# Planning a fused attention and mixture-of-experts kernel with a shared port as a lock and a margin for inputs, another seed, and softmax sums by a reduction

## The chip, the cores and the metric

One Trainium2 chip; the kernel runs on one of its cores. The metric is device time in microseconds (us) of one execution. The engines are named as in the profile: PE is TensorE, PEld its weight loads, DVE is VectorE, ACT is ScalarE, POOL is GpSimd, SP is SyncE (it issues most of the DMAs).

## What is computed

Windowed attention over 4 batches, 8 heads, 576 positions, 64 wide; its output is the input of a mixture of 8 experts (top one per token), and that of a dense block.

```python
scores = scale * np.matmul(q, k.transpose(0, 1, 3, 2))
mask = (rel >= 0) & (rel < 64)                   # rel = query position - key position
attn = exp(scores - max) / (sum(exp(scores - max)) + 1e-09)
x = (attn @ v) as 2304 rows of 512
logits = x @ w_gate + modality_bias[modality_id]
e = argmax(logits); gate_w = softmax(logits)[e]
y = gate_w * (relu(x @ w1[e]) @ w2[e])           # 8 experts, 512 -> 1024 -> 512
h = y @ w_in; out = (h - tanh(h)) @ w_out        # 512 -> 2048 -> 512
```

## The kernel before

The program has two halves. The first, `front`, does attention, routing and the experts, and it is written out in an order that a planner finds when the program is built. The second, `second`, runs the dense block over 6 chunks of 384 tokens and 16 slices each in an order fixed by hand (L1772 for `x @ w_in`, L1820 for the product with `w_out`).

The planner is the class `Flow`. Each piece of work is a Python generator that yields `Op`s: an engine (or a choice of engines) with a duration in us, the tokens it waits for, the buffers it takes. `pick` looks at every waiting `Op`, takes the engine on which something can start first, and on that engine the `Op` with the smallest priority number among those that can start within 0.05 us of the first. Priorities of 0 to 30 get a small pseudo-random addition from `nudge`, which depends on `SEED`. The generator then emits its instructions, so an engine's program order is the order in which the planner picked. On the chip every engine works through its own list in that order and waits for semaphores; the planner's own durations play no further part.

What the planner orders, with the lines that matter here:

- 16 pairs of heads (4 a batch) and 4 tails (the last 64 rows of all heads of a batch). Of a pair, PE transposes k and q (L596, L604), adds the mask and the scores (L694, L707), transposes the probabilities (L732) and multiplies with v (L746). DVE or ACT copy what PE left in PSUM (L615, L623, L380 and L382, two halves of one helper).
- The softmax, `t_soft`: DVE takes the row maximum (L774), ACT the exponentials with their sums (L777), DVE adds 1e-9 to the sums (L780) and takes reciprocals (L781), and GpSimd, or DVE, multiplies (L783). It runs 36 times.
- The routing, `route`, once a batch, when all heads of the batch are done: PE forms the logits (L885, then L902, with `lt` their transpose); DVE adds the bias and finds the one-hot `oh` of the expert in seven short instructions (L906, L907, L908, L919, L920, L921, L922); PE ranks the tokens (L926, L927, where L927 waits for `oh`); DVE and GpSimd build a table (L941 to L992).
- The experts, in five units of up to 504 tokens: unit 0 is early and needs only the first batch's table, unit 1 the third's, units 2 to 4 that of all. A unit is 96 matmuls of the first layer (L1365) and 96 of the second (L1385). `t_wsplit` cuts the weights in two parts, `wh` (L380 or L382) and `wl` (L1340), `t_hid` gives the hidden rows `hh` (L1396) and `hl` (L1399). They have the largest priority numbers, so they fill in where attention leaves an engine free.
- `t_conv` turns the dense block's weights from float64 words into float32 (L1455 to L1482), from about 150 us on.

Of the kernel before, what the change touches and what calls it, by code (L numbers as in the profile page):

```python
# [56 lines left out]
SPACE = 2.0  # L57
NUDGE, SEED = 1.0, 179
CONV0 = 14
# [85 lines left out]
class Op:  # L145
    def __init__(self, eng, deps=(), rings=(), bank=None, prio=None, wire=0.0, lag=1.6, nb=1, bias=None):
        self.eng = eng if isinstance(eng, dict) else {eng[0]: eng[1]} if eng else {}
        self.deps, self.rings, self.bank, self.prio, self.wire = deps, rings, bank, prio, wire
        self.lag, self.nb, self.bias = lag, nb, bias

# [5 lines left out]
class Flow:  # L156

    LAG = dict(PE=0.3, DVE=0.17, ACT=0.2, POOL=0.15, SP=0.0)
    BIAS = dict(DVE=0.2)
    LOOK = 0.05  # L160

    def __init__(self):
        self.free = dict(PE=5.8, DVE=5.0, ACT=5.0, POOL=8.0, SP=1.6)
        self.wire, self.th, self.n, self.floor = 0.0, [], 0, 0.0
        self.bank = [Tok(0.0) for _ in range(8)]

# [32 lines left out]
    def nudge(self, n):  # L199
        x = (n + 1) * (2 * SEED + 1) * 2654435761 % 2**32  # L200
        return NUDGE * ((x ^ x >> 15) * 2246822519 % 2**32 >> 8) / 2**24

    def pick(self):
        best = {}
        for th in self.th:
            op = th[3]
            t = self.ready(op)
            if t is None:
                continue
            t = max(t, th[4])  # L210
            if not op.eng:
                return None, t, th
            bias = op.bias or self.BIAS
            e = min(op.eng, key=lambda e: max(self.free[e], t) + op.eng[e] + (len(op.eng) > 1) * bias.get(e, 0.0))
            best.setdefault(e, []).append((max(self.free[e], t), th))
        assert best, "nothing can go on"
        e = min(best, key=lambda e: min(s for s, _ in best[e]))
        lo = min(s for s, _ in best[e]) + self.LOOK
# [4 lines left out]
        s, th = min((x for x in best[e] if x[0] <= lo), key=lambda x: prio(x[1]))  # L223
        return e, s, th

    def run(self):
        while self.th:
            e, s, th = self.pick()
            op, r = th[3], Done()
            r.e, r.s, r.rel = e, s, [g.take() for g in op.rings]  # L230
            r.t = s
            if e:
                end = s + op.eng[e]
                self.free[e] = end
                r.t = end + self.LAG[e]
                if op.wire:
                    self.wire = max(self.wire, end) + op.wire
                    r.t = self.wire + op.lag
                elif e == "POOL" and op.lag > 2:
                    r.t = end + op.lag  # L240
            else:
                th[4] = s
            if op.bank is not None:
                free = sorted((b for b in op.bank if self.bank[b].t is not None), key=lambda b: self.bank[b].t)
                r.bs = free[: op.nb]
                r.bts = [Tok() for _ in r.bs]
                r.bt = r.bts[0]
                for b, t in zip(r.bs, r.bts):
                    self.bank[b] = t
            r.tok = Tok(r.t)  # L250
            self.step(th, r)


class Kernel:
# [132 lines left out]
    def front(self):  # L387
# [93 lines left out]
    def t_load(self):  # L481
# [19 lines left out]
        def v(pi):  # L501
            b, hp = divmod(pi, 4)
            h0 = 2 * hp
            r = yield Op(("SP", 1.3), rings=[R["va"]], prio=1.25 * pi + 0.3, wire=W256)
            va = at.tile([128, 4, 2, 64], F32, name="va", bufs=NVA)
            for h in range(2):
                nc.sync.dma_start(va[:, :, h, :], ap["v"][b, h0 + h, 0:512, :].rearrange("(c p) d -> p c d", p=128))
            vb = at.tile([128, 3, 2, 64], F32, name="vb", bufs=NVA)
            self.raw["v", pi] = va, vb, r.rel[0]
            self.tk("va", pi).t = r.t  # L510
            here = Tok(r.t + 1.0)
            r = yield Op(("POOL", 0.53), [here], prio=1.25 * pi - 0.5)
            nc.gpsimd.tensor_copy(vb[0:64], va[0:64, 1:4])
            t, e, d = (r.t, "DVE", 0.35) if self.behind(r) else (r.t, "POOL", 0.53)
            r = yield Op((e, d), [here], prio=-30 if e == "POOL" else 1.25 * pi - 0.5)
            self.eng(r).tensor_copy(vb[64:128], va[64:128, 0:3])
            self.tk("vb", pi).t = max(t, r.t)
# [250 lines left out]
    def t_soft(self, key, ps, P, bs, tok):  # L768
        nc, at = self.nc, self.at
        r = yield Op(("DVE", 0.6), [tok])  # L770
        nm = at.tile([128, 4], F32, name="nm", bufs=8)
        sm = at.tile([128, 4], F32, name="smm", bufs=8)
# [6 lines left out]
        r = yield Op(("DVE", 0.36), [r.tok])  # L779
# [97 lines left out]
    def route(self, b):  # L877
# [25 lines left out]
        r = yield Op(("DVE", 0.65), [r.tok])  # L903
        Lg = rt.tile(sh, F32, name="Lg")
# [8 lines left out]
        te = r.tok  # L913
        r = yield Op(("DVE", 1.1))
        cand = rt.tile(sh, F32, name="cand")
# [22 lines left out]
        tp = r.tok  # L938
        r = yield Op(("DVE", 0.53), [te])
        se = rt.tile([128, n], F32, name="se")  # L940
# [3 lines left out]
        for t in range(t0, t1):  # L944
            self.flow.add(self.t_after(r.tok, self.t_xrow(t)), -6 + 0.01 * t)
        r = yield Op(("DVE", 0.35), [tp])
        ccn = rt.tile([128, E], F32, name="ccn")
# [4 lines left out]
        elif b == B - 1:  # L952
            self.flow.add(self.unit_table(r.tok), -9)
        r = yield Op(("DVE", 1.4), [tp])
        rk = cand
# [269 lines left out]
    def t_late(self):  # L1225
        we, self.es_we = self.pool("we", 1)
        for n in range(NLATE):
# [9 lines left out]
            self.nc.scalar.activation(self.wH[t], w, AF.Copy)  # L1237
            r = yield Op(dict(DVE=0.75, POOL=1.3), [r.tok], bias=dict(POOL=0.6))
            self.eng(r).tensor_tensor(lo, w, self.wH[t].bitcast(F32), op=ALU.subtract)
# [90 lines left out]
    def t_wsplit(self, i, s, w, tok, rel):  # L1330
        nc, mo, R = self.nc, self.mo, self.rings
        r = yield Op(dict(ACT=0.52, DVE=0.46), [tok], [R["wh"]])
# [108 lines left out]
    def t_conv(self, n, t):  # L1441
# [17 lines left out]
        tb = r.tok  # L1459
        yield Op(("DVE", 0.5), [ta])  # L1460
        v.tensor_scalar(x, x, bits(0x38000000), bits(0x47EFFFFF), op0=ALU.max, op1=ALU.min)
        yield Op(("DVE", 0.5))
        v.tensor_scalar(a, a, 0x07FFFFFF, 3, op0=ALU.bitwise_and, op1=ALU.logical_shift_left)
        r = yield Op(("DVE", 0.68))
        v.scalar_tensor_tensor(a, hi, -0x40000000, a, op0=ALU.bitwise_and, op1=ALU.bitwise_or)
        rr.t = max(r.t, tb.t)
        if t not in self.wH:
            r = yield Op(("POOL", 1.5), [r.tok, tb])
# [4 lines left out]
        r = yield Op(("POOL", 1.5), [r.tok, tb], [R["cw"]])  # L1473
        rw = r.rel[0]
# [502 lines left out]
```

## Time and profile before

| | |
|---|---|
| runs | 743.62, 743.67, 746.39 us; median 743.67 |
| the profiled execution | 745.83 us, span from first to last instruction 744.0 us |
| TensorE's mean granted clock | 0.992 of full speed |
| busy, share of the span | PE 97%, PEld 84%, DVE 78%, ACT 68%, POOL 43% |
| chain of work that ended last, by engine | PE 86%, DVE 7%, POOL 2%, issue 2%, ACT 1%, DMA 1% |
| HBM | 103 GB/s over the span |

The profile gives for each engine the time it was busy and, for each idle stretch, what ended it. Ends of matmuls are modelled, so PE can look busy without running at its full rate; the rate is read from how long equal pieces of work take in the chain of waits. Times in a timeline row are start and duration; what stands in brackets is how long the engine had been idle and who ended that.

### The profile page before, as it was taken

How to read it: one execution, taken by the hardware profiler on the slowest of the kernel's cores; microseconds unless marked ns; L12 is line 12 of the kernel's file. 1: busy time of each engine (PE TensorE's matmuls, PEld its weight loads, DVE VectorE, ACT ScalarE, POOL GpSimd, SP SyncE). 2: the span in 40 equal slices, each digit the busy share in tenths (PEclk: the TensorE clock that was granted, in tenths of full speed). 3: DMA queues.
4: the chain of work that ended last, by engine and by line, in shares of the span. 5: the costliest groups of instructions: out<-in, count | busy, mean ns of one | idle time of the engine just before them, and what ended most of it. 6: DMA issues, size and time to landing. Idle time of an engine off the chain costs nothing.

```text
span 744.0 us, 14477 instructions
## 1 busy us (share of the span) xinstructions
PE 723.3 (97%) x4939; PEld 627.8 (84%) x4939; DVE 581.5 (78%) x1095; ACT 507.9 (68%) x1222; POOL 322.3 (43%) x355
## 2 busy tenths in 40 slices
PE   7998999999999999999999999999999999999995
PEld 4777877788888887899998989899998989999894
DVE  6999985999999877758999996767677676767663
ACT  5887885667666555638887777667676766767672
POOL 6786673543433422214685442334244333424222
PEclk9999999999999999999999999999999999999998
DMA  8987864688786875641010110101010000001001
GB/s 187 221 199 160 201 177 121 206 246 247 225 258 212 261 244 175 187 131 30 1 43 1 43 33 11 39 7 41 1 44 22 21 15 30 23 0 43 1 0 47
DMA packets 119249, 77.30 MB, mean 104 GB/s; under 512 B 54968, under 2 KB 112332, under 8 KB 119166
## 3 DMA queue, kind: packets, MB, share of 16 engines
q1 hardware_dynamic: 114822, 66.38, 31.9%
q0 software_dynamic: 3264, 9.63, 4.1%
q8 instruction: 41, 0.67, 0.4%
q10 hardware_dynamic: 1080, 0.28, 0.2%
q14 instruction: 42, 0.34, 0.2%
HBM read 62.10 MB, written 14.16 MB: 103 GB/s over the span
## 4 chain that ended last, share of the span: by engine, by line
PE 86%; DVE 7%; POOL 2%; issue 2%; ACT 1%; DMA 1%; DVEq 0%; POOLq 0%; ACTq 0%
PE ps_g L1772 26%; PE ps_q L1820 26%; PE bank L1385 14%; PE bank L1365 12%; PE bank L746 1%; PE bank L1290 1%; DVE nm L774 1%; ACT P L777 1%; PE bank L732 1%; DMA kr<-in_k 1%; PE bank L707 1%; PE bank L857 1%; PE bank L596 1%; DVE kT L623 1%; DVE qT L615 1%
## 5 line engine op out<-in xcount | busy, mean ns | idle before, releaser
L1803 POOL TENSOR_TENSOR gl<-gv,gh 128x384 fp32r<-128x384 f32 x95 | 101.9, 1073 | 168.6 <-ACT gh L1802 166.6
L1820 PE MATMUL ps_q<-H,gl 128*128 128x512 f32 x288 | 114.0, 396 | 0.0
L1790 DVE SCALAR_TENSOR_TENSOR gv<-gu,ps_g 128x384 f32<-128x384 f32 x94 | 51.7, 550 | 79.5 <-ACT gt L1785 79.2
L1820 PE MATMUL ps_q<-H,gh 128*128 128x512 f32 x288 | 113.4, 394 | 0.0
L1802 ACT ACTIVATE gh<-gv 128x384 fp32r<-128x384 f32 x96 | 50.2, 523 | 91.0 <-issue 85.4
L1794 DVE COPY_PREDICATED gv<-gm,gt 128x384 f32<-128x384 int32 x96 | 77.2, 804 | 11.0 <-DVE gv L1793 1.4
L1793 DVE SCALAR_TENSOR_TENSOR gv<-gs,gv 128x384 f32<-128x384 f32 x96 | 68.9, 718 | 10.7 <-DVE gv L1792 0.9
L1340 DVE TENSOR_TENSOR wl<-raw,wh 128x512 fp32r<-128x512 f32 x74 | 62.3, 860 | 12.8 <-ACT wh L380 8.8
L1820 PEld LDWEIGHTS ps_q<-H,gl 128*128 128x128 f32 x288 | 54.1, 188 | 12.9 <-DVE gl L1803 0.3
L1786 ACT ACTIVATE gs<-gu,pa 128x384 f32<-128x384 f32 x96 | 59.2, 616 | 7.2 <-DVE gv L1792 7.2
L1787 ACT ACTIVATE gs<-gu,pa 128x384 f32<-128x384 f32 x96 | 59.0, 614 | 7.2 <-DVE gv L1793 7.2
L1792 DVE SCALAR_TENSOR_TENSOR gv<-gs,gv 128x384 f32<-128x384 f32 x96 | 61.9, 645 | 0.0
L1820 PEld LDWEIGHTS ps_q<-H,gh 128*128 128x128 f32 x288 | 54.1, 188 | 9.0 <-ACT gh L1802 0.2
L1789 ACT ACTIVATE gm<-gu,pth 128x384 f32<-128x384 f32 x96 | 58.4, 609 | 0.0
L1791 DVE TENSOR_TENSOR gt<-ps_g,gt 128x384 f32<-128x384 f32 x94 | 51.7, 550 | 0.0
L1784 ACT ACTIVATE gu<-ps_g 128x384 f32<-128x384 f32 x94 | 44.4, 472 | 1.6 <-PE ps_g L1772 1.6
L1785 ACT ACTIVATE gt<-ps_g 128x384 f32<-128x384 f32 x94 | 45.3, 482 | 0.0
L1396 ACT ACTIVATE hh<-bank 128x504 fp32r<-128x504 f32 (+1 forms) x40 | 22.1, 553 | 29.5 <-PE bank L1365 29.5
L380 ACT ACTIVATE ys<-bank 128x504 f32<-128x504 f32 (+1 forms) x20 | 11.1, 556 | 44.8 <-PE bank L1385 32.9
L1365 PE MATMUL bank<-xh,wh 128*128 128x504 f32 (+1 forms) x160 | 41.5, 379 | 0.0
L1365 PE MATMUL bank<-xl,wh 128*128 128x504 f32 (+1 forms) x160 | 41.4, 378 | 0.0
L380 ACT ACTIVATE wh<-raw 128x512 fp32r<-128x512 f32 x68 | 41.1, 624 | 0.0
(479 smaller groups left out, 2060.5 us busy)
## 6 DMA issues: line engine op xcount, KB each, us to landing
raw<-in_w SPq DMA_DIRECT2D x80, 256.0 KB
craw<-in_win SPq DMA_DIRECT2D x16, 512.0 KB
craw<-in_wout SPq DMA_DIRECT2D x16, 512.0 KB
va<-in_v SPq DMA_DIRECT2D x32, 128.0 KB
yd<-ys SPq DMA_DIRECT2D x16, 252.0 KB
yr<-yd SPq DMA_DIRECT2D x20, 192.0 KB
kr<-in_k SPq DMA_DIRECT2D x11, 256.0 KB
qr<-in_q SPq DMA_DIRECT2D x10, 256.0 KB
```

Of the source, the lines that this page charges most:

```text
L1340: self.eng(r).tensor_tensor(lo, w, hi.bitcast(F32), op=ALU.subtract)
L1365: nc.tensor.matmul(ps, wt[:, k, :], xt[:, k, :n], start=(k == 0 and q == 0), stop=(k == 3 and q == 2))
L1385: nc.tensor.matmul(ps, wt[:, k % 4, :], h, start=(q == 0), stop=(q == 3 * NF1 - 1))
L1772: nc.tensor.matmul(ps, w[:, c, :], x[:, c, :], start=(c == 0 and i == 0), stop=(c == 3 and i == 2))
L1786: nc.scalar.activation(s1, u, AF.Square, bias=self.pa1)
L1787: nc.scalar.activation(s2, u, AF.Square, bias=self.pa2)
L1789: nc.scalar.activation(m, u, AF.Relu, bias=self.pth)
L1792: nc.vector.scalar_tensor_tensor(v, s1, b1, v, op0=ALU.add, op1=ALU.mult)
L1793: nc.vector.scalar_tensor_tensor(v, s2, b2, v, op0=ALU.add, op1=ALU.mult)
L1794: nc.vector.copy_predicated(v, m.bitcast(I32), t)
L1803: (nc.vector if last else nc.gpsimd).tensor_tensor(gl, v, gh.bitcast(F32), op=ALU.subtract)
L1820: self.nc.tensor.matmul(self.po[t], g[:, t * 128 : t * 128 + 128], w, start=(f == 0 and i == 0), stop=(f == NF2 - 1 and i == 2),)
```

## The change

Four things are edited.

1. `SEED` is 78 instead of 179, so the pseudo-random additions to priorities differ.
2. [...] An `Op` on DVE can be marked `lock`; such an `Op` isn't started while a GpSimd `Op` runs, and a GpSimd `Op` isn't started while a marked DVE `Op` runs. With the lock, the durations that the planner assumes for many DVE steps get smaller. Routing steps, weight splits, conversions and one copy of v are marked.
3. `pick` compares an engine's candidates by the time at which they can start or, if later, by the time their inputs are there plus a margin (0.7 us on PE, 0.2 us on DVE and GpSimd). Work whose inputs have been ready for longer goes first.
4. The sums of the softmax. Eight tiles of 128x4x2 are set to 1e-9 once, at the start; ACT writes its sum into the first element of each pair, and a DVE TENSOR_REDUCE over the pair takes the place of the TENSOR_SCALAR that added 1e-9. The reciprocal stays.

```diff
-NUDGE, SEED = 1.0, 179
+NUDGE, SEED = 1.0, 78
...
+    WAIT = dict(PE=0.7, DVE=0.2, POOL=0.2)
...
+    def held(self, e, op, t):
+        o = dict(DVE="POOL", POOL="DVE").get(e)
+        if o is None or (e == "DVE" and not op.lock):
+            return t
+        a, b = self.hold[o]
+        return b if a < t + op.eng[e] and t < b else t
...
-            e = min(op.eng, key=lambda e: max(self.free[e], t) + op.eng[e] + (len(op.eng) > 1) * bias.get(e, 0.0))
-            best.setdefault(e, []).append((max(self.free[e], t), th))
+            s = {e: self.held(e, op, max(self.free[e], t)) for e in op.eng}
+            e = min(s, key=lambda e: s[e] + op.eng[e] + (len(s) > 1) * bias.get(e, 0.0))
+            best.setdefault(e, []).append((max(s[e], t + self.WAIT.get(e, 0.0)), s[e], th))
...
+                if e == "POOL" or (e == "DVE" and op.lock):
+                    self.hold[e] = s, end
...
+        self.sums, self.nsum = [at.tile([128, 4, 2], F32, name=f"sum{i}") for i in range(8)], 0
...
+        for t in self.sums:
+            nc.vector.memset(t, 1e-9)
...
-            t, e, d = (r.t, "DVE", 0.35) if self.behind(r) else (r.t, "POOL", 0.53)
-            r = yield Op((e, d), [here], prio=-30 if e == "POOL" else 1.25 * pi - 0.5)
+            t, e, d = (r.t, "DVE", 0.42) if self.behind(r) else (r.t, "POOL", 0.53)
+            r = yield Op((e, d), [here], lock=True, prio=-30 if e == "POOL" else 1.25 * pi - 0.5)
...
-            nc.scalar.activation(P[:, j, :], ps[:, j, :], AF.Exp, bias=nm[:, j : j + 1], accum_out=sm[:, j : j + 1])
+            nc.scalar.activation(P[:, j, :], ps[:, j, :], AF.Exp, bias=nm[:, j : j + 1], accum_out=sm[:, j, 0:1])
-        nc.vector.tensor_scalar(sm, sm, 1e-9, None, op0=ALU.add)
-        nc.vector.reciprocal(rc, sm)
+        nc.vector.tensor_reduce(rc, sm, op=ALU.add, axis=AX.X)
+        nc.vector.reciprocal(rc, rc)
...
-        r = yield Op(("DVE", 1.1))
+        r = yield Op(("DVE", 0.95), lock=True)
...
-        by = dict(DVE=0.8, POOL=1.2) if i < NEARLY else dict(DVE=0.8)
-        r = yield Op(by, [r.tok], [R["wl"]], bias=dict(POOL=LATE))
+        by = dict(DVE=0.62, POOL=1.2) if i < NEARLY else dict(DVE=0.62)
+        r = yield Op(by, [r.tok], [R["wl"]], bias=dict(POOL=LATE), lock=True)
```

The order of nearly every engine's instructions in the first half differs. Two places are shown. In the changed kernel line numbers are 12 to 16 higher (L906 is L922, L922 is L938, L902 is L918, L1365 is L1381).

The first is DVE in the routing of the second batch, from a copy of v to the one-hot `oh`; `nm` is a softmax maximum, `smm` a softmax sum. Before:

```order
L516 COPY vb<-va 64x384
L774 TENSOR_REDUCE nm<-bank_1536 128x4
L780 TENSOR_SCALAR smm<-smm 128x4
L781 RECIPROCAL rc<-smm 128x4
L516 COPY vb<-va 64x384
L906 TENSOR_TENSOR Lg<-bank_1613,btok 128x40
L907 TENSOR_REDUCE mx<-Lg 128x5
L908 TENSOR_TENSOR Lg<-Lg,mx 128x40
L919 TENSOR_SCALAR cand<-Lg 128x40
L920 TENSOR_TENSOR cand<-cand,iomp 128x40
L921 TENSOR_REDUCE idx<-cand 128x5
L922 TENSOR_TENSOR oh<-iom_190,idx 128x40
```

And in the changed kernel, from the third routing instruction on (a single copy of v stands directly ahead of the first, L922):

```order
L924 TENSOR_TENSOR Lg<-Lg,mx 128x40
L799 TENSOR_TENSOR P_111<-P_111,rc 128x512
L796 TENSOR_REDUCE rc<-sum_142 128x4
L797 RECIPROCAL rc<-rc 128x4
L790 TENSOR_REDUCE nm<-bank_1619 128x4
L638 COPY kT_106<-bank_1588 128x4x2x64
L394 COPY PT<-bank_1660 128x512
L935 TENSOR_SCALAR cand<-Lg 128x40
L936 TENSOR_TENSOR cand<-cand,iomp 128x40
L937 TENSOR_REDUCE idx<-cand 128x5
L938 TENSOR_TENSOR oh<-iom_206,idx 128x40
```

Six instructions of attention now stand inside the routing chain, between its third and its fourth instruction.

The second place is PE in the routing of the third batch, from the logits' transpose (`ltT`) to the ranking matmul that waits for `oh` (weights `tri`); `xh` and `xl` are rows of expert unit 0, `wh` and `wl` its weights, `P_112` probabilities. Before:

```order
L902 MATMUL bank_2144<-sel,ltT 128x8 x5
L732 MATMUL bank_2157<-idF,P_112 128x64
...
L604 MATMUL bank_2180<-idF,qr_96 128x128 x4
...
L707 MATMUL bank_2193<-kT_106,qT_105 64x128
...
L746 MATMUL bank_2230<-PT,va 64x64 x4
...
L926 MATMUL bank_2253<-cc,ones 128x40
L927 LDWEIGHTS tri
```

In the changed kernel:

```order
L918 MATMUL bank_2269<-sel,ltT 128x8 x5
L1381 MATMUL bank_2231<-xl,wh 128x504 x4
L1381 MATMUL bank_2231<-xh,wl 128x504 x2
...
L722 MATMUL bank_2305<-kT_104,qT_103 64x128
...
L761 MATMUL bank_2336<-PT,va 64x64 x4
...
L1381 MATMUL bank_2231<-xh,wl 128x504 x2
L942 MATMUL bank_2367<-cc,ones 128x40
L943 LDWEIGHTS tri
```

Eight expert matmuls now stand between the logits and the ranking; a transpose of probabilities and one of q left this place. Over the whole first half, 62 of unit 0's 96 first-layer matmuls stand ahead of the last batch's L902, against 40 before. On DVE, ahead of the last batch's routing, there are 4 more `wl` products, 2 more `hl`, 1 more cast of `wh` and 2 more copies of 128x512, and 1 copy of v and 1 row scaling fewer; of two copies the shape differs.

## Rows read from the trace of the kernel before

**Rows 1.** The page, part 1: busy time by engine.
```profile
PE 723.3 (97%) x4939; PEld 627.8 (84%) x4939; DVE 581.5 (78%) x1095; ACT 507.9 (68%) x1222; POOL 322.3 (43%) x355
```

**Rows 2.** Busy time by stage: PE, PEld, DVE, ACT, POOL, granted clock, DMA.
```profile
20.00:64.00 44.00, 41.98 (x802) 35.14 (x802) 40.56 (x113) 37.39 (x160) 33.52 (x52) 1.00 0.84 194
64.00:84.00 20.00, 18.02 (x295) 15.52 (x295) 18.50 (x50) 16.25 (x65) 14.78 (x20) 0.91 0.68 178
84.00:106.00 22.00, 20.39 (x323) 15.92 (x323) 20.14 (x57) 17.16 (x62) 13.66 (x20) 0.92 0.85 191
106.00:146.00 40.00, 38.12 (x372) 30.21 (x371) 29.20 (x84) 24.84 (x68) 20.18 (x24) 1.00 0.56 171
170.00:334.00 164.00, 164.00 (x822) 139.06 (x821) 135.59 (x218) 98.71 (x185) 51.94 (x40) 1.00 0.70 215
```

**Rows 3.** The chain that ended last, 145 to 340 us: start, duration, what.
```profile
170.14 21.97 PE bank L1365 x96
...
215.91 21.97 PE bank L1365 x96
...
333.43 6.24 PE ps_g L1772 x36
```

**Rows 4.** PE's longest waits, 6 to 146 us: total, times, longest one.
```profile
PE bank L927 <- DVE oh L922: 3.8, 3, 1.9
```

**Rows 5.** Timeline of PE at the second and third routing: start, duration, line, [idle before].
```profile
67.78 0.81 PE L902 MATMUL bank<-sel,ltT 128*128 128x8 f32 x6
...
72.73 0.18 PE L927 MATMUL bank<-oh,tri 128*128 128x40 bf16 x1 [1.91 <-DVE oh L922]
...
100.32 0.18 PE L927 MATMUL bank<-oh,tri 128*128 128x40 bf16 x1 [1.49 <-DVE oh L922]
```

**Rows 6.** Busy time and granted clock around and after these two waits.
```profile
71.00:79.00 8.00, 6.27 (x76) 5.69 (x76) 7.40 (x24) 5.68 (x14) 5.95 (x9) 0.79 0.48 134
98.00:106.00 8.00, 6.51 (x71) 4.97 (x65) 6.98 (x26) 5.90 (x18) 5.65 (x8) 0.79 0.51 135
```

**Rows 7.** Timeline of DVE at the second and third routing.
```profile
67.03 2.00 DVE L516 COPY vb<-va 64x384 f32<-64x384 f32 x1
...
72.48 0.20 DVE L922 TENSOR_TENSOR oh<-iom,idx 128x40 bf16<-128x40 f32 x1
...
98.39 0.47 DVE L919 TENSOR_SCALAR cand<-Lg 128x40 f32<-128x40 f32 x1
...
99.36 0.91 DVE L922 TENSOR_TENSOR oh<-iom,idx 128x40 bf16<-128x40 f32 x1
```

**Rows 8.** Timeline of POOL at the same two places.
```profile
67.76 1.04 POOL L783 TENSOR_TENSOR cvr<-cvr,rc 128x512 f32<-128x512 f32 x1
...
98.89 2.55 POOL L1340 TENSOR_TENSOR wl<-raw,wh 128x512 fp32r<-128x512 f32 x2
```

**Rows 9.** Timeline of DVE at the start.
```profile
6.57 0.69 DVE L623 COPY kT<-bank 128x512 f32<-128x512 f32 x1 [0.54 <-PE bank L596]
```

**Rows 10.** Groups of DVE instructions, 0 to 340 us: busy us, mean ns.
```profile
L780 DVE TENSOR_SCALAR smm<-smm 128x4 f32<-128x4 f32 x36 | 11.1, 309 | 1.5 <-ACT P L777 1.2 <-ACT cvr L777 0.3
...
L941 DVE TENSOR_REDUCE se<-ex 128x5 f32<-128x40 f32 x4 | 0.7, 175 | 0.0
```

**Rows 11.** Lines L780 and L941 each: duration in ns, least, median, most.
```profile
L780 DVE TENSOR_SCALAR smm<-smm x36: 140/170/1057, 11.2 to 116.5; 128x4 f32<-128x4 f32 x36
...
L941 DVE TENSOR_REDUCE se<-ex x4: 165/174/188, 42.9 to 129.8; 128x5 f32<-128x40 f32 x4
```

**Rows 12.** Groups of DVE instructions, 6 to 127 us.
```profile
L1340 DVE TENSOR_TENSOR wl<-raw,wh 128x512 fp32r<-128x512 f32 x5 | 3.5, 705 | 3.4 <-PE bank L1365 3.4
```

**Rows 13.** The chain that ended last, 0 to 172 us.
```profile
86.37 0.87 PE bank L707 x32
...
87.83 1.08 PE bank L746 x32
...
127.23 1.01 PE bank L902 x10
```

More of the change, by code (lines that the diff above doesn't have):

```diff
@@ L145, with __init__ @@
 class Op:
-    def __init__(self, eng, deps=(), rings=(), bank=None, prio=None, wire=0.0, lag=1.6, nb=1, bias=None):
+    def __init__(self, eng, deps=(), rings=(), bank=None, prio=None, wire=0.0, lag=1.6, nb=1, bias=None, lock=False):
         self.eng = eng if isinstance(eng, dict) else {eng[0]: eng[1]} if eng else {}
         self.deps, self.rings, self.bank, self.prio, self.wire = deps, rings, bank, prio, wire
-        self.lag, self.nb, self.bias = lag, nb, bias
+        self.lag, self.nb, self.bias, self.lock = lag, nb, bias, lock
 class Done:
@@ L164, in __init__ @@
         self.wire, self.th, self.n, self.floor = 0.0, [], 0, 0.0
+        self.hold = dict(DVE=(0.0, 0.0), POOL=(0.0, 0.0))
         self.bank = [Tok(0.0) for _ in range(8)]
@@ L213, in pick @@
             bias = op.bias or self.BIAS
-            e = min(op.eng, key=lambda e: max(self.free[e], t) + op.eng[e] + (len(op.eng) > 1) * bias.get(e, 0.0))
-            best.setdefault(e, []).append((max(self.free[e], t), th))
+            s = {e: self.held(e, op, max(self.free[e], t)) for e in op.eng}
+            e = min(s, key=lambda e: s[e] + op.eng[e] + (len(s) > 1) * bias.get(e, 0.0))
+            best.setdefault(e, []).append((max(s[e], t + self.WAIT.get(e, 0.0)), s[e], th))
         assert best, "nothing can go on"
-        e = min(best, key=lambda e: min(s for s, _ in best[e]))
-        lo = min(s for s, _ in best[e]) + self.LOOK
+        e = min(best, key=lambda e: min(x[0] for x in best[e]))
+        lo = min(x[0] for x in best[e]) + self.LOOK
         def prio(th):
@@ L221, in prio @@
             return (p + self.nudge(th[1]) if e != "SP" and 0 <= p < 30 else p), th[1]
-        s, th = min((x for x in best[e] if x[0] <= lo), key=lambda x: prio(x[1]))
+        _, s, th = min((x for x in best[e] if x[0] <= lo), key=lambda x: prio(x[2]))
         return e, s, th
@@ L771, in t_soft @@
         nm = at.tile([128, 4], F32, name="nm", bufs=8)
-        sm = at.tile([128, 4], F32, name="smm", bufs=8)
+        sm = self.sums[self.nsum % len(self.sums)]
+        self.nsum += 1
         rc = at.tile([128, 4], F32, name="rc", bufs=8)
@@ L776, in t_soft @@
         for j in range(4):
-            nc.scalar.activation(P[:, j, :], ps[:, j, :], AF.Exp, bias=nm[:, j : j + 1], accum_out=sm[:, j : j + 1])
+            nc.scalar.activation(P[:, j, :], ps[:, j, :], AF.Exp, bias=nm[:, j : j + 1], accum_out=sm[:, j, 0:1])
         bs.t = r.t
-        r = yield Op(("DVE", 0.36), [r.tok])
-        nc.vector.tensor_scalar(sm, sm, 1e-9, None, op0=ALU.add)
-        nc.vector.reciprocal(rc, sm)
+        r = yield Op(("DVE", 0.3), [r.tok])
+        nc.vector.tensor_reduce(rc, sm, op=ALU.add, axis=AX.X)
+        nc.vector.reciprocal(rc, rc)
         r = yield Op(dict(POOL=0.98, DVE=0.62), [r.tok], bias=dict(DVE=1.2))
@@ L902, in route @@
             nc.tensor.matmul(ps[:, i, :], self.ltT[:, w : w + 128], self.sel, start=True, stop=True, skip_group_check=True)
-        r = yield Op(("DVE", 0.65), [r.tok])
+        r = yield Op(("DVE", 0.6), [r.tok], lock=True)
         Lg = rt.tile(sh, F32, name="Lg")
@@ L938, in route @@
         tp = r.tok
-        r = yield Op(("DVE", 0.53), [te])
+        r = yield Op(("DVE", 0.5), [te], lock=True)
         se = rt.tile([128, n], F32, name="se")
@@ L945, in route @@
             self.flow.add(self.t_after(r.tok, self.t_xrow(t)), -6 + 0.01 * t)
-        r = yield Op(("DVE", 0.35), [tp])
+        r = yield Op(("DVE", 0.35), [tp], lock=True)
         ccn = rt.tile([128, E], F32, name="ccn")
@@ L953, in route @@
             self.flow.add(self.unit_table(r.tok), -9)
-        r = yield Op(("DVE", 1.4), [tp])
+        r = yield Op(("DVE", 1.2), [tp], lock=True)
         rk = cand
@@ L1237, in t_late @@
             self.nc.scalar.activation(self.wH[t], w, AF.Copy)
-            r = yield Op(dict(DVE=0.75, POOL=1.3), [r.tok], bias=dict(POOL=0.6))
+            r = yield Op(dict(DVE=0.62, POOL=1.3), [r.tok], bias=dict(POOL=0.6), lock=True)
             self.eng(r).tensor_tensor(lo, w, self.wH[t].bitcast(F32), op=ALU.subtract)
@@ L1331, in t_wsplit @@
         nc, mo, R = self.nc, self.mo, self.rings
-        r = yield Op(dict(ACT=0.52, DVE=0.46), [tok], [R["wh"]])
+        r = yield Op(dict(ACT=0.52, DVE=0.4), [tok], [R["wh"]], lock=True)
         hi, rh = mo.tile([128, DM], F32R, name="wh", bufs=NW), r.rel[0]
@@ L1459, in t_conv @@
         tb = r.tok
-        yield Op(("DVE", 0.5), [ta])
+        yield Op(("DVE", 0.42), [ta], lock=True)
         v.tensor_scalar(x, x, bits(0x38000000), bits(0x47EFFFFF), op0=ALU.max, op1=ALU.min)
-        yield Op(("DVE", 0.5))
+        yield Op(("DVE", 0.45))
         v.tensor_scalar(a, a, 0x07FFFFFF, 3, op0=ALU.bitwise_and, op1=ALU.logical_shift_left)
-        r = yield Op(("DVE", 0.68))
+        r = yield Op(("DVE", 0.61), lock=True)
         v.scalar_tensor_tensor(a, hi, -0x40000000, a, op0=ALU.bitwise_and, op1=ALU.bitwise_or)
@@ L1467, in t_conv @@
         if t not in self.wH:
-            r = yield Op(("POOL", 1.5), [r.tok, tb])
+            r = yield Op(("POOL", 1.35), [r.tok, tb])
             nc.gpsimd.tensor_tensor(self.wL[t], a, b, op=ALU.add)
@@ L1472, in t_conv @@
             return
-        r = yield Op(("POOL", 1.5), [r.tok, tb], [R["cw"]])
+        r = yield Op(("POOL", 1.35), [r.tok, tb], [R["cw"]])
         rw = r.rel[0]
@@ L1480, in t_conv @@
         nc.scalar.activation(self.flat(self.wH[t]), f, AF.Copy)
-        r = yield Op(dict(DVE=0.75), [r.tok])
+        r = yield Op(dict(DVE=0.61), [r.tok], lock=True)
         self.eng(r).tensor_tensor(self.flat(self.wL[t]), f, self.flat(self.wH[t]).bitcast(F32), op=ALU.subtract)
```

## Prediction

> **What bounds the kernel now.** I read the busy times first, then the stages, the chain of waits, and the waits of PE. PE is busy 97% of the span [rows 1]; by stage, it is idle 2.0, 2.0, 1.6 and 1.9 us in the four stages between 20 and 146 us and not at all from 170 to 334 us [rows 2]. Busy can hide slack, so the chain has to say it: there a layer of 96 expert matmuls takes 21.97 us both times shown, 0.229 us for each, and unit 1 starts 45.77 us before unit 2 [rows 3]. From 170.14 us on, the kernel is a fixed row of PE work, 573.9 of the 744.0 us, the dense block from 333.43 us included. A plan can change the end only by changing when unit 1 starts.
>
> Ahead of that the order has two kinds of PE work: attention and routing, which wait for other engines, and unit 0, which fills in. So the time is that work plus what PE loses: its waits, and time at a low clock. The longest waits are for `oh`, 3.8 us in three waits [rows 4]. [...] All that could be won between 20 and 146 us is 7.5 us of idle time and 3.4 us of clock, 10.9 us.
>
> Why was `oh` late? DVE and GpSimd got in each other's way. A copy of v took 2.00 us [rows 7] while GpSimd ran a product of 1.04 us among its other work [rows 8]; at the third routing `cand` took 0.47 and `oh` 0.91 us, the last beside a pair of GpSimd products of 2.55 us [rows 7, 8]. Undisturbed, `oh` takes 0.20 us [rows 7]. DVE itself has little room: 40.56 of 44 us, 18.50 of 20 and 20.14 of 22 us are busy up to 106 us [rows 2].
>
> **The change, part by part.**
>
> *Sums.* The 36 additions take 0.309 us on average, with a median of 0.170 and up to 1.057 us [rows 10, 11]: they wait for GpSimd. Reductions of the same kind stay between 0.165 and 0.188 us [rows 11], mean 0.175. The change saves 36 x (0.309 - 0.175) = 4.8 us of DVE. What follows is usually a GpSimd product, and where GpSimd was busy that waits anyway, so only a part lies on the path: between 0 and 4.8 us, I take a quarter, 1.2 us, since DVE is the engine waited for in some of the places and not in most. The new reduction has 8 elements where the measured one has 40; I leave that difference out.
>
> [...]
>
> The eight memsets at the start stand on DVE ahead of the first copy of k, before which DVE is idle for 0.54 us [rows 9]; I cost them at nothing. Without that cover eight short instructions could delay everything by a reduction's 0.17 us each, 1.4 us [rows 11].
>
> *The third routing.* In the new order PE has 8 expert matmuls, one pair's scores and one pair's products with v between logits and ranking: 8 x 0.229 + 0.87 + 1.08 = 3.8 us [rows 3, 13], without counting the masks. The old cover ended 1.49 us too early. On DVE, between the first routing instruction and `oh`, a large copy of q has gone and only a sum and a reciprocal remain, so that the nine need some 1.8 us at 0.2 us each (undisturbed `oh` and reductions) [rows 7, 11]. The margin of 2 us takes in one such delay as in [rows 7, 8]. I take this wait as closed, with its clock: 1.49 + 1.68 = 3.2 us.
>
> *The second routing.* PE has a tail's scores, a product with v, two transposes and a pair's scores in between, more than the one transpose and one pair's scores before. But DVE now has six instructions inside the routing chain, a product, a maximum and two copies among them. Each is of the size of a `wl` product, 0.705 us [rows 12], so 4 x 0.7 + 2 x 0.18 = 3.2 us come in. Before, 72.73 - 68.59 = 4.1 us passed from the end of the logits to the ranking [rows 5], with the copy of 2.00 us ahead of the chain. I expect a wait of about 0.4 us and no clock fall: 1.5 + 1.68 = 3.2 us gained.
>
> *What these are worth together.* 6.4 us at most from both. DVE, busy over 90% there, is next: PE's work behind the waits needs copies and maxima from DVE, and the next wait comes sooner. I count half, 3.2 us; the ends are 0 and 6.8 us.
>
> *Filling.* 22 more expert matmuls stand ahead of the last logits (62 against 40), 22 x 0.229 = 5.0 us. They win nothing by themselves: if the last L902 comes at 127.2 us as now [rows 13], the gain is 5.0 us; at 132.3 us it is nothing. It is the same gain, seen at another place. The extra `wl` and `hl` (6 x 0.7 = 4.2 us) ahead of that routing nearly use up what the sums save.
>
> *New waits.* The margin and the lock delay something else. Of the first routing, the third instruction is followed by a sum, a reciprocal and two maxima, some 1.7 us. I put 0.3 us in the sum; the rival has the other end.
>
> *After 146 us* I expect nothing: PE is full there [rows 2, 3], and DVE with 135.6 of 164 us has room for a few `wl` products more or less. If DVE fell behind, units would start later one for one.
>
> Sum: -1.2 - 3.2 + 0.3 = -4.1 us. The profiled execution took 745.83 us, 744.0 of them span, and would take 741.7. It was 2.2 us above the median of the runs, so on the median, 743.67, the forecast is **739.6 us**. About 0.5% (3.7 us) is what a measurement of this kernel can tell from no change, so this lies just beyond it.
>
> **Rivals.**
>
> 1. *DVE paces attention, so PE's waits only move.* For it: DVE's share up to 106 us, and that its extra expert work takes the place of the time saved. Against it: 29.2 of 40 us busy from 106 to 146 us [rows 2], where that work could lie. Only 0.3 to 1 us of the sums' quarter remains: 743.0 us. It is the same case if the plan's lock does not hold on the chip because the two engines drift against the planned times; then only the sums are quicker.
>
> 2. *The routing chains get longer: slower.* Place: DVE between the third and fourth routing instruction of the first and second batch. If an inserted maximum or copy waits for PE there, all behind it wait, `oh` too, and PE, at its ranking matmul, waits for that: a circle through two queues. It decides when `oh` comes over 1.5 us behind PE's cover, the size of wait behind which the clock fell. Price: the first routing, now without a long wait, gets 1.9 + 1.7 = 3.6 us; the second has 4 us instead of 1.91, so 2.1 more; with the third unimproved that is 5.7 us, less 0.4 for the sums: 749.0 us. For it: six inserted instructions. Against: PE's cover there has grown as well.
>
> 3. *Everything closes.* Both routing places fully, 6.8 us, and half of the sums, 2.4 us: 734.5 us. Against it: DVE's share.
>
> 4. *The late stretch has slack too.* From 170 to 334 us PE's weight loads are busy 139.06 of 164 us [rows 2]; were that PE's real load, a plan that feeds it better could win up to 24.9 us: 718.8 us. Against it: two layers of 96 in exactly 21.97 us, with nothing but PE in the chain [rows 3]. [...]
>
> **How the numbers follow.** Forecast 0.42, first rival 0.28, slower 0.20, everything closes 0.08, slack late 0.02. The forecast's own range is 736 to 742 us, three quarters of it beyond 0.5%: faster 0.32 + 0.08 + 0.02 + 0.02 (edge of the first rival) = 0.44. Slower by over 0.5%, over 747.4 us: 0.19 of the 0.20. The rest, 0.37, is within 0.5%. The range for 8 in 10 reaches from 734 us, where everything closes, to 748 us, which leaves out more than half of the slower case.
>
> **What would show it.** Right: the additions' row gone and the reductions at 0.14 to 0.19 us with hardly a spread; PE's waits for `oh` under 1 us in all; granted clock 1.00 in every stage from 20 to 170 us; the last logits before 132 us; unit 1 starting near 166 us and 45.8 us between units as now. Wrong: a clock fall behind a wait at the first or second routing (rival 2), PE's idle time between 20 and 146 us still at 7 us under other names (rival 1), or a unit that takes more than 46.5 us, which would mean that DVE is late with `wl` or `hl` and that the late stretch was not safe.

## The result

The changed kernel takes **737.21 us** (median of 6 runs, 736.56 to 737.87) against 744.06 us (743.33 to 746.39, 6 runs) for the kernel before: ratio 0.9903, 95% interval 0.9888 to 0.9917, 6.9 us faster. The profiled execution took 737.28 us, its span 735.5 us, where the one before had 744.0.

The page's busy times and the stages of the changed kernel, to be read against [rows 1, 2]:

```profile
PE 721.0 (98%) x4939; PEld 625.3 (85%) x4939; DVE 568.8 (77%) x1104; ACT 509.2 (69%) x1225; POOL 318.3 (43%) x351
```

```profile
6.00:20.00 14.00, 11.73 (x198) 9.10 (x200) 9.43 (x26) 9.81 (x49) 8.58 (x16) 1.00 1.12 222
20.00:64.00 44.00, 43.17 (x830) 35.98 (x834) 37.92 (x115) 38.35 (x166) 34.06 (x55) 1.00 0.81 192
64.00:84.00 20.00, 19.33 (x336) 16.59 (x333) 19.02 (x55) 17.01 (x71) 15.15 (x20) 1.00 1.10 236
84.00:106.00 22.00, 22.00 (x361) 16.89 (x360) 20.44 (x62) 18.89 (x73) 12.35 (x19) 1.00 0.55 142
106.00:146.00 40.00, 38.90 (x315) 31.25 (x314) 29.65 (x89) 23.77 (x50) 18.15 (x20) 1.00 0.63 187
164.00:328.00 164.00, 164.00 (x824) 139.41 (x823) 137.44 (x220) 103.95 (x195) 51.90 (x40) 1.00 0.72 219
```

From 20 to 146 us PE is idle for 0.83 + 0.67 + 0.00 + 1.10 = 2.6 us, before 7.5. The granted clock is 1.00 in every stage; before it was 0.91 and 0.92 in two of them. DVE is no emptier from 64 to 106 us than before, 39.46 against 38.64 of 42 us: the work that PE no longer waits for has come in more tightly.

The chain of work that ended last, the expert units, to be read against [rows 3]:

```profile
161.74 0.46 PE bank L1381 x2
162.31 21.67 PE bank L1381 x94
207.82 21.97 PE bank L1381 x96
253.64 21.97 PE bank L1381 x96
299.94 12.64 PE bank L1381 x96
325.38 6.25 PE ps_g L1788 x36
```

Unit 1 starts at 161.74 us, before at 170.14: 8.4 us earlier, and the span is 8.5 us shorter. From there on next to nothing has changed: a layer still takes 21.97 us, and 207.82 to 253.64 is 45.8 us for a unit (unit 1 itself takes 46.1, 161.74 to 207.82). So the whole gain was made ahead of unit 1. The 8.4 us are those of two single executions: the profiled one before took 745.83 us, 1.8 us above the median of 744.06, so about 1.5 us of them are more than the 6.9 us between the medians, and no profile says which.

PE's waits from 6 to 146 us, the longest of them, against [rows 4]:

```profile
PE bank L722 <- DVE qT L630: 1.2, 1, 1.2
PE bank L1306 <- DVE T L1021: 0.8, 1, 0.8
PE bank L873 <- ACT xr L879: 0.7, 1, 0.7
PE bank L747 <- POOL P L799: 0.6, 2, 0.3
```

The wait for `oh`, 3.8 us before, is gone. What happened to it at the second routing stands in the timelines of PE and then DVE:

```profile
66.56 1.18 PE L918 MATMUL bank<-sel,ltT 128*128 128x8 f32 x10
...
71.74 1.23 PE L722 MATMUL bank<-kT,qT 64*64 64x128 f32 x32
72.95 0.18 PE L943 MATMUL bank<-oh,tri 128*128 128x40 bf16 x1
```

```profile
67.93 0.36 DVE L531 COPY vb<-va 64x384 f32<-64x384 f32 x1
68.32 0.20 DVE L922 TENSOR_TENSOR Lg<-bank,btok 128x40 f32<-128x40 f32 x1
...
68.90 0.69 DVE L799 TENSOR_TENSOR P<-P,rc 128x512 f32<-128x512 f32 x1
...
71.56 0.19 DVE L935 TENSOR_SCALAR cand<-Lg 128x40 f32<-128x40 f32 x1
...
72.25 0.20 DVE L938 TENSOR_TENSOR oh<-iom,idx 128x40 bf16<-128x40 f32 x1
```

The ranking (L943) starts at 72.95 us, where it had started at 72.73 [rows 5], and `oh` is hardly earlier, at 72.25 us against 72.48 [rows 7]. But the ranking has no bracket, PE did not wait: a pair's scores end where it begins. From the end of the logits to the start of `oh` it takes 72.25 - 67.74 = 4.5 us, before 72.48 - 68.59 = 3.9 us. The routing chain was not shortened; its length was covered. The one copy of v ahead of it took 0.36 us, where the first of two had taken 2.00 [rows 7], and the six inserted instructions, from 68.90 to 71.56 us, took that time for work that had to be done anyway.

The new reduction of the sums, by its line, against the additions in [rows 11]:

```profile
L796 DVE TENSOR_REDUCE rc<-sum x36: 129/150/162, 11.9 to 112.2; 128x4 f32<-128x8 f32 x36
```

### The profile page after: what moved, and what is told of

It is laid out like the page before. It is cut to its first block, busy times and chain, and to the rows that moved or that the text cites. A ratio compares the mean times of both kernels' runs of the same rounds, so it can differ in the third digit from the quotient of the medians.

```text
span 735.5 us, 14501 instructions
## 1 busy us (share of the span) xinstructions
PE 721.0 (98%) x4939; PEld 625.3 (85%) x4939; DVE 568.8 (77%) x1104; ACT 509.2 (69%) x1225; POOL 318.3 (43%) x351
## 4 chain that ended last, share of the span: by engine, by line
PE 88%; DVE 6%; ACT 1%; DMA 1%; issue 1%; POOL 1%; POOLq 0%; SPq 0%; DVEq 0%; ACTq 0%
PE ps_g L1788 27%; PE ps_q L1836 26%; PE bank L1401 14%; PE bank L1381 13%; PE bank L722 1%; PE bank L1306 1%; DVE nm L790 1%; PE bank L761 1%; DMA kr<-in_k 1%; PE bank L747 1%; DMA va<-in_v 1%; ACT P L793 1%; PE bank L873 1%; PE ps_q L1788 1%; PE bank L901 1%
## 5 line engine op out<-in xcount | busy, mean ns | idle before, releaser
L1356 DVE TENSOR_TENSOR wl<-raw,wh 128x512 fp32r<-128x512 f32 x78 | 64.7, 848 | 13.3 <-ACT wh L392 12.5
L1809 DVE SCALAR_TENSOR_TENSOR gv<-gs,gv 128x384 f32<-128x384 f32 x96 | 65.8, 686 | 10.7 <-ACT gt L1801 0.5
L1808 DVE SCALAR_TENSOR_TENSOR gv<-gs,gv 128x384 f32<-128x384 f32 x96 | 60.4, 629 | 0.0
L392 ACT ACTIVATE wh<-raw 128x512 fp32r<-128x512 f32 x72 | 43.5, 626 | 0.0
L1381 PE MATMUL bank<-xl,wh 128*128 128x504 f32 (+1 forms) x160 | 41.5, 376 | 0.0
L1381 PE MATMUL bank<-xh,wh 128*128 128x504 f32 (+1 forms) x160 | 41.1, 375 | 0.0
L1381 PE MATMUL bank<-xh,wl 128*128 128x504 f32 (+1 forms) x160 | 40.8, 373 | 0.0
```

Source lines behind the costliest of these rows:

```text
L1381: nc.tensor.matmul(ps, wt[:, k, :], xt[:, k, :n], start=(k == 0 and q == 0), stop=(k == 3 and q == 2))
L1808: nc.vector.scalar_tensor_tensor(v, s1, b1, v, op0=ALU.add, op1=ALU.mult)
L1809: nc.vector.scalar_tensor_tensor(v, s2, b2, v, op0=ALU.add, op1=ALU.mult)
```

## The experiments

Every ratio is to the kernel before, run beside it on the same chip. They ran in groups, each on one chip, and the kernel before differs between the groups: 744.06 us beside the changed kernel, 745.75 beside experiments 1 to 4, 745.43 beside 5 to 8, 743.85 beside 9 to 12. That is 0.26%, so a comparison between groups holds, at that size, only if a chip shifts all kernels alike, which nothing here tests. Experiments 3, 8 and 11 add work whose result nothing reads; none leaves work out.

### 1. The sums alone

The kernel before with the new sums; its order of instructions stays.

```diff
-        nc.vector.tensor_scalar(sm, sm, 1e-9, None, op0=ALU.add)
-        nc.vector.reciprocal(rc, sm)
+        nc.vector.tensor_reduce(rc, sm, op=ALU.add, axis=AX.X)
+        nc.vector.reciprocal(rc, rc)
```

> The kernel before with the new softmax sums alone; planner, seed and so the order of every engine's instructions stay. Theory (the gain of 6.9 us comes from the new order, which closes PE's waits for oh and with them the clock falls): the reductions take 0.15 us without spread, DVE loses 5 us of busy time, and 0 to 2 us of it arrive, 742 to 744 us; both waits for oh and both clock falls stay. Rival (the freed DVE is the gain): 4 us or more, 740 us or less, and the waits for oh shrink below 1 us.

Measured: 742.31 us, ratio 0.9947 (0.9933 to 0.9961). That is 0.53%, 3.9 us of 744: more than half of the whole gain from one edit. That is inside the theory's range, and in its profile the waits for `oh` are still there; the clock is the surprise. PE's timeline, then the stages:

```profile
41.88 0.18 PE L931 MATMUL bank<-oh,tri 128*128 128x40 bf16 x1 [0.52 <-DVE oh L926]
...
71.87 0.18 PE L931 MATMUL bank<-oh,tri 128*128 128x40 bf16 x1 [1.23 <-DVE oh L926]
...
99.94 0.18 PE L931 MATMUL bank<-oh,tri 128*128 128x40 bf16 x1 [1.45 <-DVE oh L926]
```

```profile
42.00:44.00 2.00, 2.00 (x41) 1.98 (x40) 1.72 (x10) 1.96 (x10) 1.32 (x2) 0.53 0.57 122
44.00:46.00 2.00, 2.00 (x43) 1.83 (x43) 1.79 (x6) 0.84 (x2) 1.45 (x3) 0.62 0.40 90
64.00:84.00 20.00, 16.68 (x291) 14.05 (x284) 17.57 (x47) 16.55 (x64) 14.83 (x19) 1.00 0.73 180
84.00:106.00 22.00, 20.34 (x359) 15.90 (x359) 20.15 (x57) 17.21 (x61) 14.05 (x21) 1.00 0.85 189
```

Waits of 1.23 and 1.45 us are followed by no fall (clock 1.00 in both stages), although the second is as long as the 1.49 us in [rows 5]; the one fall stands at 42 to 46 us, behind a wait of 0.52 us. Neither fall that was expected to stay is there. The link from a long wait to a clock fall, which the prediction's second rival uses, does not hold as it stood there.

### 2. The order alone

The changed kernel with the sums of before: the diff of experiment 1 turned round.

```diff
-        nc.vector.tensor_reduce(rc, sm, op=ALU.add, axis=AX.X)
-        nc.vector.reciprocal(rc, rc)
+        nc.vector.tensor_scalar(sm, sm, 1e-9, None, op0=ALU.add)
+        nc.vector.reciprocal(rc, sm)
```

> The changed kernel with the old sums (addition by TENSOR_SCALAR); the order of the changed kernel stays. Theory (order): most of the gain stays, 738 to 740 us, additions again spread up to 1 us. Rival (sums): 741 us or more.

Measured: 740.69 us, 0.9921 (0.9904 to 0.9937), between the two ranges expected. The new order, seed included, is worth 0.79% without the sums, and the sums on top of it only 0.9921 - 0.9903 = 0.18%, which is within the intervals. The two do not add up, and one reason may be in the group of the additions, here in the new order, against [rows 10]:

```profile
L792 DVE TENSOR_SCALAR smm<-smm 128x4 f32<-128x4 f32 x36 | 9.2, 255 | 1.3 <-ACT P L789 1.2
```

In the new order the same additions take 255 ns on average where they took 309: part of what drew them out is gone already.

### 3. PE filled ahead of the ranking

The kernel before, with 9 and 7 idle matmuls ahead of the second and third ranking, to cover the wait for `oh`.

```diff
         pr, bk = self.bt(r, 128, n, E), r.bt
+        for _ in range({1: 9, 2: 7}.get(b, 0)):
+            nc.tensor.matmul(
+                self.bt(r, 128, 4, 128), self.ones, self.ones[:, None, :].to_broadcast([128, 4, 128]), start=True, stop=True,
+            )
```

> The kernel before with 9 and 7 idle matmuls of 512 columns put on PE ahead of the ranking matmul of the second and third routing; their result is overwritten, the waits for oh stay as long but PE is busy in them. Theory (the clock falls follow PE's idle stretches and cost 1.7 us each on the path): granted clock 1.00 from 64 to 106 us, 3 us less, 740 to 741.5 us. Rival (PE's slow stretches are hidden behind DVE, which paces attention): clock 1.00 too, but 743 to 744 us. Third outcome: the clock falls all the same, then it was not the idle stretch; no change.

Measured: 745.82 us, 0.9998 (0.9989 to 1.0006), the "no change" of the third outcome, but with the falls at the two places gone and one at another. PE's timeline and two stretches:

```profile
70.97 3.89 PE L927 MATMUL bank<-ones 128*128 128x512 bf16 x9
...
74.95 0.18 PE L931 MATMUL bank<-oh,tri 128*128 128x40 bf16 x1
```

```profile
44.00:46.00 2.00, 2.00 (x56) 2.00 (x52) 1.85 (x9) 2.00 (x10) 0.77 (x2) 0.71 0.02 4
64.00:84.00 20.00, 19.40 (x303) 14.89 (x304) 17.05 (x47) 15.47 (x61) 14.54 (x20) 1.00 0.67 177
```

The fill was too much: an idle matmul took 0.43 us, nine 3.89 us, and the ranking came at 74.95 us instead of 72.73. Where PE was filled the clock stayed at 1.00, but a fall stood at 42 to 46 us. Sixteen matmuls, 6.9 us, bought 3.2 us of idle time and 1.7 us of clock (table below). So it does not tell apart whether the waits cause the falls; a fill of the right length was not tried.

### 4. The new planner with the old seed

```diff
-NUDGE, SEED = 1.0, 78
+NUDGE, SEED = 1.0, 179
```

> The changed kernel with seed 179 instead of 78. Theory (the planner's lock and margin give the better order whatever the seed): 735 to 740 us, no wait for oh above 1 us. Rival (the seed was a lucky draw): 741 to 746 us, with PE waits or clock falls at new places.

Measured, for the changed kernel with this edit: 744.4 us, 0.9979 (0.9967 to 0.9991), as the rival had it. With the same sums and the same seed the old planner had 0.9947: here the lock and the margin made the kernel slower, and the seed matters more than they do.

### 5, 10. The old planner with seed 78, with and without the new sums

```diff
-NUDGE, SEED = 1.0, 179
+NUDGE, SEED = 1.0, 78
```

Experiment 10 is the kernel before with only this; experiment 5 has the sums of experiment 1 too.

> The kernel before with the new sums and seed 78: the planner without lock and margin. Theory (seed and planner act together, an order is a draw): anywhere from 738 to 746 us, with the sums alone at 742.3. Rival (seed 78 is good by itself): 737 to 738 us, as the changed kernel. Rival (lock and margin are the gain): 742 to 746 us.

> The kernel before with seed 78 alone: old planner, old sums. Theory (seed 179 was a poor order for the chip, most of the gain is the other draw): ratio 0.991 to 0.995, that is 2 to 5 us less than its old sums give at seed 179. Rival (the sums are most of it, and the seed adds little): 0.997 or more.

Measured: the seed alone 740.99 us, 0.9964 (0.9950 to 0.9978); with the sums 738.82 us, 0.9912 (0.9896 to 0.9929). Experiment 10 lies between its two ranges; experiment 5 is in its wide one and just above the 737 to 738 us of the seed alone. The stage of the third routing in experiment 10, and PE's waits for `oh` in experiments 10 and 5:

```profile
84.00:106.00 22.00, 21.32 (x359) 17.00 (x361) 19.18 (x56) 18.09 (x64) 12.57 (x19) 1.00 0.78 182
```

```profile
PE bank L927 <- DVE oh L922: 0.5, 2, 0.3
```

```profile
PE bank L931 <- DVE oh L926: 0.5, 1, 0.5
```

With nothing but another seed the long waits for `oh` are gone and the clock is 1.00. Under the old planner seed and sums add up, 0.9964 x 0.9947 = 0.9911, and without lock or margin they come to within 0.1% of the changed kernel. The reverse, lock and margin at seed 78 without the sums, is experiment 2, and it is not settled: its 0.9921 and the 0.9964 of experiment 10 are apart by more than their intervals, but the times, from different groups, are 740.69 and 740.99 us, and unit 1 starts later in experiment 2 (165.42 against 163.99 us).

### 6, 7, 12. Other seeds

The changed kernel with seed 1 (experiment 6), experiment 1 with seed 1 (experiment 7) and with seed 2 (experiment 12).

```diff
-NUDGE, SEED = 1.0, 179
+NUDGE, SEED = 1.0, 1
```

> The changed kernel with seed 1, not chosen by anybody. If the new planner is better by itself: 736 to 740 us. If seed 78 was selected: 741 to 746 us, like seed 179 with 744.4.

> The kernel before with the new sums and seed 1. If the new planner is better by itself, this is 3 us or more above the new planner's seed 1; if the order is a draw, the two lie within 3 us in either direction.

> The kernel before with the new sums and seed 2, a third free draw of the old planner. If 179 is the odd one out, 0.990 to 0.993; if the spread of draws is as wide as that from 179 to 78, anywhere from 0.988 to 0.996. Below 0.988 it would beat both kernels.

Measured, ratios of all runs with the new sums:

| planner | seed 179 | seed 78 | seed 1 | seed 2 |
|---|---|---|---|---|
| old | 0.9947 | 0.9912 | 0.9918 | 0.9980 |
| new | 0.9979 | 0.9903, 0.9905 | 0.9931 | not run |

Medians in us for the three of this group: 739.65, 739.09, 742.28. Experiments 6 and 7 lie within 3 us of each other, which was to mean that an order is a draw; seed 2 came out above both ranges expected, so 179 is not the odd one out. The intervals are about 0.0016 to either side. Between seeds the old planner spreads over 0.7%, some seven tenths of the changed kernel's gain of 0.97% and more than the two planners differ at any seed. Over the three common seeds the means are 0.9926 for the old and 0.9938 for the new. That the new planner is the better one is not shown; an order is a draw, and 78 is a good one under both.

### 8, 11. DVE loaded again

Experiment 1 with one idle reciprocal for each softmax, behind its own (experiment 8) or ahead of it (experiment 11). The edit shown is that of experiment 11.

```diff
         nc.vector.tensor_reduce(rc, sm, op=ALU.add, axis=AX.X)
+        nc.vector.reciprocal(at.tile([128, 4], F32, name="idle", bufs=8), nm)
         nc.vector.reciprocal(rc, rc)
```

> The sums-only kernel (742.3 us) with 36 more reciprocals on DVE, one behind each softmax's own, into a tile that nobody reads: 36 x 0.18 = 6.4 us of DVE, outside the softmax chain, order otherwise as before. Theory (DVE's throughput paces attention, which is why filling PE brought nothing and freeing DVE did): 4 us or more, 746 us or above. Rival (the sums paid because they shorten the softmax's chain): 742 to 744 us.

> The sums-only kernel with the same 36 idle reciprocals as the loaded one (ratio 0.9967), now between the reduction and the softmax's own reciprocal, so inside the chain. Theory (what counts is when DVE is held up, not in which chain): 0.995 to 0.998, as with the other place. Rival (the softmax's chain is what the time hangs on): 0.999 or more, the sums' gain gone.

Measured: 0.9967 (0.9956 to 0.9978), 742.84 us, and 0.9979 (0.9964 to 0.9995), 742.07 us; experiment 11 is in its theory's range, while the 746 us or more of experiment 8's did not come. The row of the idle instruction in experiment 11:

```profile
L785 DVE RECIPROCAL idle<-nm 128x4 f32<-128x4 f32 x36 | 6.0, 166 | 0.0
```

DVE gets back 5.3 and 6.0 us, about the 5.7 us that the sums had freed, and by the ratios between 0.2 and 0.3% of the time comes back, not the whole 0.53% (for experiment 11 the interval reaches close to it). So DVE's total is probably not all that counts. It may be that the additions' rare long times, up to 1.06 us [rows 11], cost more than the same time spread evenly; that is argued, not shown.

The two places make no difference beyond the intervals, but they do not separate load from chain as was expected of them. GpSimd's waits for the softmax's reciprocals (total, times, longest), 6 to 146 us, first in experiment 1, then in experiment 8:

```profile
POOL P L787 <- DVE rc L785: 11.6, 8, 3.3
```

```profile
POOL P L788 <- DVE idle L786: 9.2, 6, 3.3
```

Also where the idle reciprocal stands behind the softmax's own, the profile puts GpSimd's waits down to it. So both places lie inside the chain, as far as the profile tells, and a load outside it was not tried.

### 9. The changed kernel again

No edit; it ran beside experiments 10 to 12.

> The changed kernel once more, beside the others of this job and on their chip. Ratio 0.988 to 0.992 as before. If lock and margin add something to seed and sums, it stays below the old planner's 0.9912 with seed 78 and the same sums by more than the intervals; theory now: it doesn't.

Measured: 736.87 us, 0.9905 (0.9889 to 0.9922), the same as the first time.

### What all fourteen profiles say together

For each kernel's profile: the start of unit 1; PE's idle time from 6 us to there and the time lost to a granted clock under 1.00, both added up over stretches of 4 us; and what is left of the start without the two (in experiment 3 also without the idle matmuls' 6.9 us).

| kernel | unit 1 starts, us | idle | clock | left |
|---|---|---|---|---|
| before | 170.14 | 10.6 | 3.4 | 156.1 |
| 1 sums alone | 168.44 | 10.3 | 1.7 | 156.4 |
| 2 order alone | 165.42 | 9.0 | 0.0 | 156.4 |
| 3 PE filled | 170.95 | 7.4 | 1.7 | 154.9 |
| 4 new planner, 179 | 168.21 | 10.9 | 1.7 | 155.6 |
| 5 old planner, 78 | 164.28 | 7.6 | 0.0 | 156.7 |
| 6 new planner, 1 | 163.72 | 7.4 | 0.0 | 156.3 |
| 7 old planner, 1 | 164.13 | 7.5 | 0.0 | 156.6 |
| 8 DVE loaded | 168.23 | 10.9 | 0.0 | 157.3 |
| 9 changed again | 161.33 | 5.2 | 0.0 | 156.1 |
| 10 seed 78 alone | 163.99 | 7.8 | 0.0 | 156.2 |
| 11 loaded in chain | 167.66 | 10.5 | 1.7 | 155.5 |
| 12 old planner, 2 | 167.13 | 10.7 | 0.0 | 156.4 |
| changed | 161.74 | 4.9 | 0.0 | 156.8 |

Experiment 3 apart, the last column holds within 1 us of 156.4: whatever was edited, unit 1 starts when some 156.4 us of PE work plus PE's idle time plus its lost clock are over. The column says that the work stays the same, and so where the time went; it does not say what took the idle time away. The changed kernel's 8.4 us are 5.7 us of idle time and 3.4 us of clock, less 0.7 us in the last column. Clock is lost in pieces of 1.7 us, none, one or two of them to a profile. Of the six profiles with over 10 us of idle time four have such a piece, of the seven others (experiment 3 apart, which has one) none; experiments 8 and 12 lost none with 10.9 and 10.7 us idle.

Two things limit what one profile can say. From the start of the last unit to the end the spans differ by up to 2.8 us (434.6 us in experiment 8, 437.4 in experiment 10), which no edit touches; the changed kernel's two profiles have 435.6 and 435.9. And a profile is one run: that of experiment 1, 744.55 us, was the slowest of its six, whose granted clocks from 0.995 to 0.998 go with times from 744.55 down to 740.64 (correlation -0.97). For the kernel before the same correlation is -0.08, -0.60 and -0.64 over its 23, 13 and 20 runs, so there the clock explains a part at most.

## Why the prediction was right, and where it was not

The forecast was 739.6 us, 4.1 us faster; measured were 737.2 us, 6.9 us faster by the medians beside each other. The side and the range hold, and so does the frame: a fixed row from unit 1 on, and ahead of it work, idle time and clock. What was too small is the sum; unit 1, expected near 166 us, started at 161.74.

**The routing places.** Right: no wait for `oh`, and the clock at 1.00 up to 170 us. The inserted instructions took 2.66 us where 3.2 were reckoned, and even the 0.4 us left over at the second routing did not come. At the third the nine on DVE took 2.2 us (97.06 to 99.28 us) where 1.8 were reckoned, `oh` 0.70 of them, which the margin took in. The step that failed is "I count half, 3.2 us". The next wait did not come sooner: besides the 3.4 us that the two waits took, PE lost 2.3 us less elsewhere (idle 10.6 to 4.9 us is 5.7 in all), 0.8 of it from 6 to 20 us, a stage that the sum left out. The upper end that I gave, 6.8 us for the two waits and the clock around them (1.91 + 1.49 + 2 x 1.68) [rows 5, 6], would have been nearer; the order alone gave 0.79%, 5.9 us.

**The clock.** The 1.68 us of clock in each of the two sums, 3.4 us for both, are 8 us x 0.21, from the mean of 0.79 over the 8 us around each wait [rows 6]. As a term it was real: ahead of unit 1, 3.4 us were lost in the one profile before and none in the two of the changed kernel. But such waits do not bring it by themselves: experiment 1 has both, of 1.23 and 1.45 us, and no fall at either, and a fall elsewhere. Whether less idle time lowers the chance of a fall, or the new order avoids it otherwise, stays open.

**The sums.** A reduction takes 0.151 us, not 0.175, so DVE is freed of 36 x (0.309 - 0.151) = 5.7 us instead of 4.8. The reductions stand at 0.129 to 0.162 us, just below the 0.165 to 0.188 us of the row they were costed from [rows 11]. That the additions waited for GpSimd shows in the trace of the kernel before: each of the 14 that took over 0.2 us ended 0.02 to 0.03 us after a GpSimd instruction, and the longest ran for 1.06 us from 116.53 us, beside a GpSimd product of 1.04 us from 116.52. Whether a shared port, as in the title, is what held them up, no run shows. That "a quarter" lies on the path fits only what the sums add to the new order (0.18%, 1.3 us against 1.2), and that is luck as far as the intervals go; by themselves they are worth 3.9 us, two thirds of the freed time. How it reaches the end is not shown: in experiment 1's profile PE's idle time fell by only 0.3 us, and one clock fall fewer made the rest of its 1.7 us, and from experiment 10 to 5 unit 1 doesn't start earlier at all, though the ratios differ by 0.52% and the times by 2.2 us. Between those two profiles the difference lies behind the start of the last unit (437.4 against 435.1 us), in a part that the sums do not touch.

**What was credited to the planner.** The prediction read two places and had them closed by the new order, without asking which edit made it. Old planner, seed 78 and sums give 0.9912 against 0.9903 and 0.9905. In the profiles lock and margin do save another 2.4 to 2.7 us of idle time at this seed (7.6 against 4.9 and 5.2). By the ratios 0.5 to 0.7 us of that is left, within their intervals; by the medians of the different groups it is 1.6 to 2.0 us. At seed 1 they save 0.1 us, and at 179 nothing.

**Filling.** Right: 62 expert matmuls stand ahead of the last logits instead of 40, and these still start at 123.95 us where they had started around 127 [rows 13]. 22 x 0.229 = 5.0 us more work and some 3 us less time comes near the 8.4 us once more.

**New waits and the memsets.** The largest wait is now 1.2 us (PE for `qT`, 0.6 before), so 0.6 us more where the sum has 0.3, but it came in a total that fell. The memsets cost nothing to be seen: behind them DVE waited 0.83 us for PE ahead of the first copy of k (0.54 before [rows 9]).

**After 146 us.** Right: units at 45.8 us, PE busy 164 of 164 us. There was one change of price behind that cover: the conversions' first step (L1463, now L1479), 32 times, went from a mean of 610 to 758 ns, 19.5 to 24.3 us of DVE. PE did not wait for it.

**The rivals.** DVE pacing (743.0): no; PE's idle time did not move, it went. Slower chains (749.0): six instructions in the chain lengthened no wait. Everything closes (734.5) was, beside the forecast, the nearest to what happened, given 0.08. Slack in the late stretch (718.8): the weight loads are busy 139.41 of 164 us, as before, and the units take what they took; none of the runs tried to win the 24.9 us, so that they can be had is not shown.

## What to carry to other kernels

When a change replaces a planned order, take its cheap parts alone before crediting the clever one: here another seed and one small edit gave 0.88 of 0.97%, and four seeds spread over 0.7%. A wait for a chain can be closed by covering the chain, with the chain itself no shorter; so look at what the waiting engine has ahead of the wait, not only at the late one. And check an accounting (fixed work + idle + lost clock) over several variants: where the remainder stays constant, it is the sum of all the idle time that a new order changes, not the two places that one happens to read.

## What was not expected of the hardware

- A TENSOR_REDUCE of 128x4 from 128x8 took 129 to 162 ns in all 36 places (mean 151 ns; 152 ns in experiments 1, 8 and 11), while a TENSOR_SCALAR of 128x4 in their place took up to 1057 ns [rows 11]. No reduction was drawn out, though 14 of the 36 ran wholly beside a single GpSimd instruction, at the same 129 to 162 ns.
- Falls of the granted clock (to 0.50 of full speed from 75 to 77 us in the kernel before; 0.53 and 0.62 over the two stretches from 42 to 46 us in experiment 1) came behind a wait as short as 0.52 us, did not come behind one of 1.45 us, and differed between kernels with the same order of instructions (experiment 1 and the kernel before).
- An idle matmul of 128x128 weights by 512 bf16 columns (experiment 3) took 0.43 us at a granted clock of 1.00; an expert matmul of 504 columns takes 0.229 us [rows 3]. Why is not shown.
